# A list-scheduled Longformer-and-mixer kernel: a later second gather and other costs in its planner

## Chip, cores and metric

The kernel runs on one core of one Trainium2 chip. The metric is the device time of one execution in microseconds (us). Before the change it is 309.04 us, the median of three runs (308.41 to 309.81).

## The reference

Inputs are q, k and v (8 batches, 8 heads, S = 576 positions, D = 64), eight global positions, and four weight matrices. All of it is float32 in DRAM.

```python
scores = scale * np.matmul(q, k.transpose(0, 1, 3, 2))
mask = np.abs(pos[:, None] - pos[None, :]) <= window          # window = 32
mask = mask | is_global[:, None] | is_global[None, :]
scores = np.where(mask, scores, -1000000000.0)
attn = softmax(scores);  x = (attn @ v) as (B, S, H * D)      # 576 x 512 per batch
h = np.maximum(xt @ w_tok1, 0.0) @ w_tok2                     # 576 -> 256 -> 576, xt is x transposed
u = x + h.transpose(0, 2, 1)
h2 = np.maximum(u @ w_ch1, 0.0) @ w_ch2                       # 512 -> 1536 -> 512
return (u + h2).astype(np.float32)
```

## The kernel before, in words

**Stages.** The eight batches b = 0..7 go through the same stages, in float16 with float32 sums on TensorE (PE). q, k and v are loaded (lines 504 to 528) and cast on ScalarE (ACT) or VectorE (DVE) (L533, L536, L548); v also gets a copy shifted by 64 rows (L556). q and k are transposed, on PE for batches 0 to 2 (L568, with the copies to qT at L571 and to kT at L576, and for the last 64 positions L587, L589, L591), by DMA afterwards. Scores of the band are matmuls L675, their exponentials L685 on ACT, masked at L691 on DVE, with the columns of the global keys copied at L694; the global rows are L705 to L714. Sums and products with v are L722, L728, L742 and L755, divided and written to x by L782 to L791. The token MLP is L805 (relu L809 to L814), then L823 with the sum u at L836 and L839. The channel MLP needs u transposed: L850 on PE with the copy to uT at L852 for b < 3, a DMA transpose later. Its first product is L868 (twelve blocks j of four matmuls; relu L860 on ACT or L862 on DVE) and for the last 64 rows of two batches L880; its second product is L911. L919 adds u to that and writes one of three output buffers `osb` in turn, and L922 stores the buffer from GpSimd's queue. An L919 thus waits for the store of three tiles before.

**Two gathers.** The key and query rows at the global positions are fetched by indirect DMAs on GpSimd (POOL, L489). The first gather serves batches 0 to 3. The second serves batches 4 to 7: two DMAs each into `g_q` and `g_k`, cast to float16 at L619 (on DVE or ACT), transposed on PE at L623. Those transposes stand at about 130 us in the program.

**What sets the order.** Nothing runs when `op()` (L96) is called; it records an operation with the engines that may do it and their costs, a priority, what it reads and writes, its PSUM keys, and for a DMA a tuple `dma = (work, weight, lag, packets)` and a delay `late`. `run()` (L119) is a list scheduler: again and again it takes for each engine the earliest candidates, of these the one with the lowest priority number, and so fixes each engine's program order, the engine where two are allowed, and the PSUM bank (`slot`). `flow` and `land` model the three queues (G for GpSimd, S for SyncE, A for ACT), which share the DMA engines by weight. After the landing so found a consumer's data count as there only `late + LATE` later (from 36 us on). A matmul group whose `mode` differs from the one before is charged 0.095 us more. All of this happens while the kernel is built; on the chip each engine runs its fixed list and waits on semaphores.

Of the kernel before, what the change touches and what calls it, by code (L numbers as in the profile page):

```python
# [16 lines left out]
NT = 5  # L17
# [10 lines left out]
def kernel(  # L28
# [84 lines left out]
        ops.append(dict(opts=opts, pri=pri, fn=fn, deps=deps, ps=ps, new=new, dma=dma, mode=mode, late=late, behind=set(behind)))  # L113
        return i

    RING, LATE = 4096, 2.0
    LAT = {"P": 0.16, "A": 0.1, "V": 0.09, "G": 0.05, "S": 0.0, "K": 0.0}

    def run(free, look, hop, warm_until):  # L119
# [73 lines left out]
        while ready:  # L193
            cand = {}
            for i in ready:
                o = ops[i]
                t0, sl = 0.0, None
                if o["new"]:
                    sl = slot(o["new"][0], len(o["new"][1]), max([free["P"]] + list(at[i].values())))
                    if sl is None:  # L200
                        continue
                    t0 = max(t0, max(x[0] for x in sl))
                best = None
                for k, (e, c) in enumerate(o["opts"]):
                    st = max([free[e], t0] + [f + (hop if x != e else 0.0) for x, f in at[i].items()])
                    if o["dma"]:
                        ln, z = lanes["G" if e == "G" else "S"], filled["A" if e == "K" else e]
                        if len(ln) >= 8:
                            st = max(st, max(ln[-8], ln[-7], ln[-6]) + 2.5 if e == "A" else ln[-8])
                        room, x = RING - o["dma"][3], len(z)  # L210
                        while x and room >= z[x - 1][1]:
                            room -= z[x - 1][1]
                            x -= 1
                        if x:
                            st = max(st, z[x - 1][0])
                    if e == "P" and o["mode"] != mode:
# [12 lines left out]
            e, (st, _, i, c, sl) = pick  # L229
            o = ops[i]  # L230
            if e == "P":
                gap, spare = st - free["P"], [k for k in range(8) if (banks[k][1] is None or not open_uses[banks[k][1]]) and banks[k][0] <= free["P"]]
                if st < warm_until and gap > 0.52 and spare:
                    warm(min(spare, key=lambda k: (banks[k][0], k)), int((gap - 0.3) / (0.22 if st < 12.0 else 0.12)))
                mode = o["mode"]
            if o["new"]:
                kind, keys, shape, dt = o["new"]
                for key, (_, k) in zip(keys, sl):
                    home[key] = [k, k + 1] if kind == "S" else [k]
                    for z in home[key]:  # L240
                        banks[z] = (0.0, key)
                    ps_tile[key] = view(k, shape, dt)
            o["fn"](e)
            free[e] = st + c
            f = st + c + LAT[e]
            if o["dma"]:
                work, size, lag, packets = o["dma"]
                q = "A" if e == "K" else e
                if e == "A":
                    free["S"] = max(free["S"], st) + 0.9 * o["dma"][3] / 1024  # L250
                drain(min(f, min(free[x] for x in "GSA")))
                f = land(q, f, work, size, i)
                filled[q].append((f, packets))
                f += lag
                lanes["G" if e == "G" else "S"].append(f)
                f += o["late"] + (LATE if st > 36.0 else 0.3)
            fin[i] = f
            log.append((st, f, e, i, max(o["deps"], key=lambda x: fin[x]) if o["deps"] else None))
            ready.discard(i)
            for key in o["ps"]:  # L260
                open_uses[key] -= 1
                for z in home[key]:
                    banks[z] = (max(banks[z][0], f + hop), key)
            for u in users[i]:
# [227 lines left out]
                )  # L492
        return f

    TURN, STORE = (0.75, 256, 0.35, 544), (0.78, 2048, 0.8, 128)

# [7 lines left out]
    def load_qk(b, ti, hs, pri, opts, after=(), late=0.0, ):  # L504
        def f(e):
            ENG[e].dma_start(
                out=(lq, lk)[ti][:, hs].rearrange("p h i d -> p h (i d)"),
                in_=(q, k)[ti][b, hs, 0 : S - LAST, :].rearrange("h (p i) d -> p h (i d)", i=4),
            )
        ps_ = range(hs.start // 2, hs.stop // 2)  # L510
        op(opts, pri, f, w=[("l", ti, p) for p in ps_], dma=(0.75 * len(ps_), 4096, 2.0, 64) if opts[0][0] == "G" else ((0.75 if b else 0.95) * len(ps_), 1024, 1.2, 256 * len(ps_)), behind=after, late=late)

    def load_rest(b, pri, opts, after=(), late=0.0, ):
        for t, ten in enumerate((q, k)):
            def f(e, t=t, ten=ten):
                ENG[e].dma_start(
                    out=lr[LAST * t : LAST * t + LAST], in_=ten[b, :, S - LAST : S, :].rearrange("h p d -> p h d")
                )
            op(opts, pri, f, w=[("lr", t)], dma=(0.5, 4096, 2.0, 32) if opts[0][0] == "G" else (0.78 if b else 0.9, 256, 1.2, 512), behind=after, late=late)

    def load_v(b, pri, opts, after=(), late=0.0, ):
        for c in range(NT):
            def f(e, c=c):
                r0, r1, j0 = vrows(c)
                ENG[e].dma_start(
                    out=lv[r0:r1, c], in_=v[b, :, j0 : j0 + (r1 - r0), :].rearrange("h p d -> p h d")
                )
            op(opts, pri + 0.1 * c, f, w=[("lv", c)], dma=(0.9 if 0 < c < NT - 1 else 0.7, 4096, 2.0, 64) if opts[0][0] == "G" else (1.05 if 0 < c < NT - 1 else 0.8, 256, 1.2, 1024), behind=after, late=late)

    def cast_qk(b, ti, p, pri, opts):  # L530
        def f(e):
# [201 lines left out]
    def values(b, tau, pri, split):  # L733
# [29 lines left out]
            rl += [("vo", i, tau, 0), ("vo", i, tau, 1)]  # L763
        rg = [("lf", i), ("rf", i)]
        new = ("S", [key], [P, 2, 512], F32) if full else ("M", [key], [P, 512], F32)
        cl, cg = (0.27, 0.213) if full else (0.15, 0.12)
        if split:
            op([("P", cl)], pri, lambda e: local(True, False), r=rl + [("lf", i)], ps=[key], new=new, mode="c")
            op([("P", cg)], pri - 0.5, lambda e: [glob(hf, False, True) for hf in range(2)], r=rg, ps=[key], mode="c")
# [203 lines left out]
    for b in range(B):  # L973
# [3 lines left out]
            loads(b)  # L977
        if b == 0:
            n0 = len(ops) - 1
            op([("G", 1.0)], -176, f_w1, w=["w1"], dma=(1.7, 4096, 2.0, 512), behind=[n0])  # L980
            op([("G", 1.9)], -175, f_w1l, w=["w1l"], dma=(0.4, 4096, 2.0, 64), behind=[n0])
            n2 = len(ops) - 1
            op([("G", 0.77)], -173, f_wc1(0), w=[("wc1", 0)], dma=(2.6, 4096, 2.0, 512), behind=[n0])
            op([("G", 1.0)], -174.5, f_w2, w=["w2"], dma=(2.4, 4096, 2.0, 512), behind=[n0])
            for t in (1, 2):
                op([("G", 0.77)], -173 + t, f_wc1(t), w=[("wc1", t)], dma=(2.6, 4096, 2.0, 512), behind=[n0])
            n1 = len(ops) - 1
        if b == 1:
            op([("G", 1.2)], -18, lambda e: qk_pads(1, nc.gpsimd), w=[("qT", 1, p) for p in range(NP)] + [("kT", 1, p) for p in range(NP)] + [("qTr", 1), ("kTr", 1)], behind=[n1])
# [1 line left out]
            op([("G", 0.75)], -16, f_pads2(1), w=[("x", 1, NT - 1), ("lf", 1)])  # L991
        if b < 2:
            for ti in range(2):
                op([("G", 2.7)], (-115 if ti == 0 else -174.2) if b == 0 else 70, f_gather(b, ti), r=["idx"], w=[("g32", b, ti)], dma=(0.1, 256, 1.7, 256), late=0.0 if b or ti else 2.3,
                   behind=[] if b == 0 and ti == 0 else [n2])
        casts(b)
        cast_v(b, ca - 20, [("A", 0.52), ("V", 0.57)] if b < 2 else [("A", 0.52)])
        shift_v(b, ca - 19, [slice(0, 2), slice(2, 4)] if b == 0 else [slice(0, 4)])
        if b == 0:
            loads(1, n0)  # L1000
            op([("G", 0.77)], -40, f_wc2(0), w=[("wc2", 0)], dma=(2.6, 4096, 2.0, 512), behind=[len(ops) - 1])
            load_v(1, -39, [("G", 0.87)], [len(ops) - 1])
            n0 = len(ops) - 1
            for t in (1, 2):
                op([("G", 0.77)], -36 + t, f_wc2(t), w=[("wc2", t)], dma=(2.6, 4096, 2.0, 512), behind=[n0])
        if b == 1:
            glob_rows(0, slice(1, 4), ca - 40)
        if b == 4:
# [67 lines left out]
```

## Time and profile before

| | |
|---|---|
| profiled execution, device time | 308.4 us |
| its span, first to last instruction | 306.7 us |
| mean granted PE clock | 0.987 |
| median of three other runs | 309.04 us |
| PE busy | 289.9 us |
| DVE, ACT, POOL busy | 187.3, 178.9, 60.2 us |

The rows that the prediction quotes come from five views. The page gives busy time by engine. The windows view gives, for a stretch of the span, each engine's busy time with its instruction count, then the granted PE clock, the DMA share and GB/s. The timeline of an engine gives start, length, line, operation, `output<-inputs`, shapes and count; in square brackets stands how long the engine was idle before the row and what ended that. The DMA issues of a stretch give queue, kind, KB and the time from issue to landing. The view of one tile gives the smallest, middle and largest of these landing times. Rows marked `ACTq` are instructions that ACT issues to a DMA queue.

### The profile page before, as it was taken

What the parts mean: (1) busy time and instruction counts of PE and PEld (TensorE: products, weight loads), DVE (VectorE), ACT (ScalarE), POOL (GpSimd) and SP (SyncE); (2) the same over time, 40 slices, a digit from 0 to 9 for tenths busy, and PEclk for the clock granted to TensorE, in tenths of its full rate; (3) what the DMA queues carried; (4) which work ended last, traced back from release to release, by engine and by line L of the source; (5) the groups of instructions that cost most, each with busy time, mean ns of one, the idle gap of its engine ahead of it and who ended that gap; (6) DMA issues with size and microseconds to landing.
All of it is one profiled execution on the core that took longest, in us unless ns stands there. A gap on an engine that the chain in (4) does not pass through costs nothing. (4 is left out here: it accounts for less than half of the span.)

```text
span 306.7 us, 7290 instructions
## 1 busy us (share of the span) xinstructions
PE 289.9 (95%) x2955; PEld 154.9 (51%) x2955; DVE 187.3 (61%) x411; ACT 178.9 (58%) x325; POOL 60.2 (20%) x109
## 2 busy tenths in 40 slices
PE   5969989997999989999989999999999999999995
PEld 3746645444474444544456445444555445444643
DVE  7778866668786536994476655976587357230012
ACT  3873895376986369812996089714992183305600
POOL 8489635642001010002000100002000200020000
PEclk9798999999999999999999999999999999999999
DMA  6988999999997973499946995699844411071013
GB/s 170 257 137 272 220 226 212 298 214 301 193 149 139 309 205 62 96 163 230 311 76 131 218 338 143 98 214 220 288 100 90 135 38 37 8 148 69 0 71 104
DMA packets 94820, 51.31 MB, mean 167 GB/s; under 512 B 73730, under 2 KB 90242, under 8 KB 94786
## 3 DMA queue, kind: packets, MB, share of 16 engines
q1 hardware_dynamic: 62480, 26.36, 39.9%
q0 software_dynamic: 8704, 18.45, 24.1%
q10 hardware_dynamic: 23602, 6.03, 11.1%
q8 instruction: 23, 0.38, 0.5%
q14 instruction: 11, 0.09, 0.1%
HBM read 36.11 MB, written 9.44 MB: 149 GB/s over the span
## 5 line engine op out<-in xcount | busy, mean ns | idle before, releaser
L868 PE MATMUL bank<-uT,wc 128*128 128x512 f16 x384 | 92.3, 380 | 2.5 <-DVE qT L591 1.7
L911 PE MATMUL bank<-wc,b 128*128 128x512 f16 x384 | 87.5, 379 | 0.0
L685 ACT ACTIVATE e<-bank 128x648 f16<-128x648 f32 x64 | 42.9, 740 | 44.3 <-PE bank L675 43.2
L860 ACT ACTIVATE b<-bank 128x512 f16<-128x512 f32 x87 | 51.6, 620 | 26.3 <-PE bank L868 26.2
L911 PEld LDWEIGHTS <-b 128*128 128x128 f16 x384 | 36.8, 98 | 42.6
L868 PEld LDWEIGHTS <-wc 128*128 128x128 f16 x384 | 35.1, 98 | 43.5 <-issue 4.3
L922 POOL DMA_DIRECT2D out_dram<-osb x28 | 15.6, 556 | 198.6 <-DVE osb L919 198.6
L919 DVE TENSOR_TENSOR osb<-u,bank 128x512 f32<-128x512 f16 x32 | 21.9, 686 | 46.3 <-PE bank L911 46.1
L691 DVE TENSOR_TENSOR e<-e,masku 128x1296 f16<-128x1296 f16 x28 | 23.3, 832 | 20.5 <-ACT e L685 20.1
L548 ACT CAST vsh<-lv 128x512 f16<-128x512 f32 (+3 forms) x44 | 26.6, 621 | 7.5 <-DMA lv<-in_v_dram 7.1
L836 DVE TENSOR_TENSOR u<-x,bank 128x512 f16<-128x512 f16 x30 | 18.7, 682 | 8.1 <-PE bank L823 7.8
L783 DVE TENSOR_TENSOR x<-bank,rr 128x512 f16<-128x512 f32 x32 | 22.1, 692 | 1.1
L823 PE MATMUL bank<-a,w 128*128 128x512 f16 x80 | 19.9, 379 | 0.6 <-DVE a L811 0.4
L675 PEld LDWEIGHTS <-kT 64*128 64x128 f16 x576 | 11.3, 96 | 15.2 <-issue 14.1
L805 PE MATMUL bank<-x,w 128*128 128x512 f16 x64 | 18.7, 379 | 0.0
L536 ACT CAST qk<-lk 128x512 f16<-128x512 f32 x27 | 16.6, 627 | 1.7 <-DMA lk<-in_k_dram 1.7
L742 PE MATMUL bank<-rf,lf 128*64 128x264 f16 x144 | 16.1, 294 | 1.2 <-ACT b L860 0.9
L675 PE MATMUL bank<-qT,kT 64*128 64x72 f16 x576 | 15.6, 196 | 1.2 <-ACT e L685 1.2
L536 ACT CAST qk<-lq 128x512 f16<-128x512 f32 x26 | 15.8, 624 | 1.2 <-DMA lq<-in_q_dram 0.7
L755 PEld LDWEIGHTS <-e 128*64 128x64 f16 x576 | 16.1, 115 | 0.1
L755 PE MATMUL bank<-vsh,e 128*64 128x66 f16 x320 | 15.9, 198 | 0.0
L653 DVE COPY kT<-raw 128x512 f16<-128x512 f16 x20 | 12.0, 599 | 5.2 <-DMA raw<-qk 4.9
(166 smaller groups left out, 333.8 us busy)
## 6 DMA issues: line engine op xcount, KB each, us to landing
out_dram<-osb POOLq DMA_DIRECT2D x28, 256.0 KB, 4.3
lq<-in_q_dram SPq DMA_DIRECT2D x11, 512.0 KB, 7.0
lk<-in_k_dram SPq DMA_DIRECT2D x11, 512.0 KB, 9.2
lv<-in_v_dram ACTq DMA_DIRECT2D x15, 256.0 KB, 5.4
wc<-in_moe_w_ch_dram POOLq DMA_DIRECT2D x6, 512.0 KB, 13.3
lq<-in_q_dram POOLq DMA_DIRECT2D x4, 512.0 KB, 8.5
lk<-in_k_dram POOLq DMA_DIRECT2D x4, 512.0 KB, 9.8
lv<-in_v_dram ACTq DMA_DIRECT2D x10, 192.0 KB, 5.7
```

What stands on the lines that cost most here:

```text
L536: COPY[e](out=qk[:, ti, p].rearrange("q i (r d) -> q r i d", r=2), in_=(lq, lk)[ti][:, hs])
L548: COPY[e](out=vsh[i][a:z, c, :, 0:D], in_=lv[a:z, c])
L675: nc.tensor.matmul(ps_tile[keys[z]][:, u // 3, UW * (u % 3) : UW * (u % 3) + UW], lhsT=kT[r, 64 * u : 64 * u + P], rhs=qT[r, u // 2, UW * ...
L685: op([("A", 0.595)], pri + 1, lambda e, par=par: nc.scalar.activation(out=es[i][:, 2 * p + par].rearrange("p (n u) x -> p n u x", n=3), in ...
L691: op([("V", 0.85)], pri + 2, lambda e: nc.vector.tensor_mul(out=e2, in0=e2, in1=masku.unsqueeze(1).to_broadcast([P, 2, NB, UW])), r=["mask ...
L755: nc.tensor.matmul(o[:, VW * hh : VW * hh + VW], lhsT=es[i][:, h, 2 * tau + c, x : x + 64], rhs=vod[i][:, tau, h, :] if c else vsh[i][:, t ...
L783: nc.vector.tensor_tensor(out=xo, in0=pq[:, :, :, 0:D], in1=rr.unsqueeze(3).to_broadcast([P, 2, NP, D]), op=ALU.mult,)
L823: nc.tensor.matmul(ps_tile[key], lhsT=w2[:, ch, P * tau - sh : P * tau - sh + P], rhs=a1[:, ch, :], start=(ch == 0), stop=(ch == 1 and not ...
L860: nc.scalar.activation(out=out, in_=in_, func=AF.Relu)
L868: nc.tensor.matmul(ps_tile[key], lhsT=wc1[:, cc, P * j : P * j + P], rhs=uT[:, cc, :], start=(cc == 0), stop=(cc == 3))
L911: nc.tensor.matmul(ps_tile[key], lhsT=w, rhs=wc2[:, j, :], start=(j == 0), stop=(j == NJ - 1))
L919: nc.vector.tensor_add(out=osb, in0=uls[b // 2 % 2] if last else u16s[i][:, tau], in1=ps_tile[key])
```

## The change

The second gather gets `late = 12.0` instead of 0 and both gathers a weight of 128 instead of 256, so the planner counts the second gather's data as there 12 us later. `LATE` falls from 2.0 to 1.0 for all other loads. GpSimd's loads get a weight of 100000 (`BIG`) instead of 4096 in the queue model, and the loads of v on that queue 1.35 and 1.1 us of work instead of 0.9 and 0.7. A store gets a weight of 600 instead of 2048. The half-array products of the last tile (`cl`, `cg`: products with v for 64 rows) cost 0.19 and 0.15 instead of 0.15 and 0.12. The 0.095 us of a mode switch are charged only where mode "n" is left. No operation is added or removed by hand.

```diff
-    RING, LATE = 4096, 2.0
+    RING, LATE = 4096, 1.0
...
-                    if e == "P" and o["mode"] != mode:
+                    if e == "P" and mode == "n" != o["mode"]:
                         c = c + 0.095
...
-    TURN, STORE = (0.75, 256, 0.35, 544), (0.78, 2048, 0.8, 128)
+    TURN, STORE, BIG = (0.75, 256, 0.35, 544), (0.78, 600, 0.8, 128), 100000
...
-            op(opts, pri + 0.1 * c, f, w=[("lv", c)], dma=(0.9 if 0 < c < NT - 1 else 0.7, 4096, 2.0, 64) if opts[0][0] == "G" else (1.05 if 0 < c < NT - 1 else 0.8, 256, 1.2, 1024), behind=after, late=late)
+            op(opts, pri + 0.1 * c, f, w=[("lv", c)], dma=(1.35 if 0 < c < NT - 1 else 1.1, BIG, 2.0, 64) if opts[0][0] == "G" else (1.05 if 0 < c < NT - 1 else 0.8, 256, 1.2, 1024), behind=after, late=late)
...
-        cl, cg = (0.27, 0.213) if full else (0.15, 0.12)
+        cl, cg = (0.27, 0.213) if full else (0.19, 0.15)
...
-                op([("G", 2.7)], (-115 if ti == 0 else -174.2) if b == 0 else 70, f_gather(b, ti), r=["idx"], w=[("g32", b, ti)], dma=(0.1, 256, 1.7, 256), late=0.0 if b or ti else 2.3,
+                op([("G", 2.7)], (-115 if ti == 0 else -174.2) if b == 0 else 70, f_gather(b, ti), r=["idx"], w=[("g32", b, ti)], dma=(0.1, 128, 1.7, 256), late=12.0 if b else (0.0 if ti else 2.3),
```

The other loads and weights on GpSimd's queue get `BIG` in the same way. POOL's program order is the same before and after, and SyncE's almost. The orders of PE, DVE and ACT are the same for about the first 15 us and differ in many places behind that. 9 of the relus L860 on ACT become L862 on DVE (99 to 90, and 9 to 18), and two filler matmuls (L286) on zeros are gone from PE. Three places matter below.

**Place 1, DVE between batches 1 and 2.** The program order of VectorE at about 62 to 76 us; `osb_102` to `osb_104` are the three output buffers, `qT_72` and `kT_74` the transposed q and k of batch 2, `u_1_95` the sum of batch 1, `g_q_196` the second gather's rows. Before:

```order
L836 TENSOR_TENSOR u_1_95<-x_1_92,bank 128x512 x4
L919 TENSOR_TENSOR osb_102<-u_0_94,bank 128x512
L839 TENSOR_TENSOR ul_96<-x_1_92,bank 64x512
L619 CAST g_q_196<-g_q_192 128x128
L556 COPY vod_78<-vsh_76 64x2112
L919 TENSOR_TENSOR osb_103<-u_0_94,bank 128x512
L919 TENSOR_TENSOR osb_104<-u_0_94,bank 128x512
L556 COPY vod_78<-vsh_76 64x2112
L589 COPY kT_74<-bank 128x4x64
L591 COPY qT_72<-bank 128x4x64
L571 COPY qT_72<-bank 128x4x128 x2
L919 TENSOR_TENSOR osb_102<-u_0_94,bank 128x512
```

And now, in the same place:

```order
L919 TENSOR_TENSOR osb_102<-u_0_94,bank 128x512
L536 CAST qk<-lk 128x2x4x64
L919 TENSOR_TENSOR osb_103<-u_0_94,bank 128x512
L919 TENSOR_TENSOR osb_104<-u_0_94,bank 128x512
L836 TENSOR_TENSOR u_1_95<-x_1_92,bank 128x512 x4
L839 TENSOR_TENSOR ul_96<-x_1_92,bank 64x512
L556 COPY vod_78<-vsh_76 64x2112
L589 COPY kT_74<-bank 128x4x64
L919 TENSOR_TENSOR osb_102<-u_0_94,bank 128x512
L571 COPY qT_72<-bank 128x4x128 x3
```

The cast L619 of the gather is gone from here, to about 83 us, where the one of `g_k`, which stood on ACT, follows it. Three of the four adds L919 stand ahead of the four L836, and the fourth, which writes `osb_102` for the second time, stands ahead of all three copies L571. The first L868 of batch 1 now writes the PSUM bank that this fourth add reads, and waits for it.

**Place 2, ACT between batches 2 and 3.** The program order of ScalarE at about 97 to 113 us; L525 are the loads of batch 4's v (parts of 96, 128, 128, 128 and 96 rows), which ACT issues. Before:

```order
L814 ACTIVATE a_93<-bank 128x1024
L852 COPY uT<-bank 128x4x128 x3
L525 DMA lv<-in_v_dram 96x8x64
L852 COPY uT<-bank 128x4x128
L525 DMA lv<-in_v_dram 128x8x64 x3
L525 DMA lv<-in_v_dram 96x8x64
L548 CAST vsh_76<-lv 32x8x64
L548 CAST vsh_76<-lv 64x8x64
L685 ACTIVATE e_81<-bank 128x648 x2
```

And now:

```order
L814 ACTIVATE a_93<-bank 128x1024
L525 DMA lv<-in_v_dram 96x8x64
L525 DMA lv<-in_v_dram 128x8x64 x3
L852 COPY uT<-bank 128x4x128 x2
L525 DMA lv<-in_v_dram 96x8x64
L852 COPY uT<-bank 128x4x128 x2
L548 CAST vsh_76<-lv 32x8x64
L548 CAST vsh_76<-lv 64x8x64
L548 CAST vsh_76<-lv 128x8x64 x2
L685 ACTIVATE e_81<-bank 128x648 x2
```

Four of the five issues have moved ahead of all four copies L852, and two casts more stand ahead of the exponentials. On PE, one L911 group of six matmuls has moved ahead of the last L805, one L911 of batch 2's tiles now writes the bank that the third L852 reads, and the second scores L675 of batch 3 stand ahead of its L705.

**Place 3, DVE in batch 4.** The program order of VectorE at about 144 to 153 us; `b_100` is the relu's output. Before:

```order
L691 TENSOR_TENSOR e_80<-e_80,masku 128x1296
L694 COPY eg<-e_80 128x2x5x8
L714 TENSOR_TENSOR lf_83<-lf_83,mf 128x576
L691 TENSOR_TENSOR e_80<-e_80,masku 128x1296
L694 COPY eg<-e_80 128x2x5x8
```

And now:

```order
L691 TENSOR_TENSOR e_80<-e_80,masku 128x1296
L694 COPY eg<-e_80 128x2x5x8
L714 TENSOR_TENSOR lf_83<-lf_83,mf 128x576
L862 TENSOR_SCALAR b_100<-bank 128x512
L691 TENSOR_TENSOR e_80<-e_80,masku 128x1296
L694 COPY eg<-e_80 128x2x5x8
L862 TENSOR_SCALAR b_100<-bank 128x512
L691 TENSOR_TENSOR e_80<-e_80,masku 128x1296
```

Relus of ACT now stand here on DVE: three in batch 4, and two in batch 5 in the same way.

More of the change, by code (lines that the diff above doesn't have):

```diff
@@ L510, in load_qk @@
         ps_ = range(hs.start // 2, hs.stop // 2)
-        op(opts, pri, f, w=[("l", ti, p) for p in ps_], dma=(0.75 * len(ps_), 4096, 2.0, 64) if opts[0][0] == "G" else ((0.75 if b else 0.95) * len(ps_), 1024, 1.2, 256 * len(ps_)), behind=after, late=late)
+        op(opts, pri, f, w=[("l", ti, p) for p in ps_], dma=(0.75 * len(ps_), BIG, 2.0, 64) if opts[0][0] == "G" else ((0.75 if b else 0.95) * len(ps_), 1024, 1.2, 256 * len(ps_)), behind=after, late=late)
     def load_rest(b, pri, opts, after=(), late=0.0, ):
@@ L518, in f @@
                 )
-            op(opts, pri, f, w=[("lr", t)], dma=(0.5, 4096, 2.0, 32) if opts[0][0] == "G" else (0.78 if b else 0.9, 256, 1.2, 512), behind=after, late=late)
+            op(opts, pri, f, w=[("lr", t)], dma=(0.5, BIG, 2.0, 32) if opts[0][0] == "G" else (0.78 if b else 0.9, 256, 1.2, 512), behind=after, late=late)
     def load_v(b, pri, opts, after=(), late=0.0, ):
@@ L979 @@
             n0 = len(ops) - 1
-            op([("G", 1.0)], -176, f_w1, w=["w1"], dma=(1.7, 4096, 2.0, 512), behind=[n0])
-            op([("G", 1.9)], -175, f_w1l, w=["w1l"], dma=(0.4, 4096, 2.0, 64), behind=[n0])
+            op([("G", 1.0)], -176, f_w1, w=["w1"], dma=(1.7, BIG, 2.0, 512), behind=[n0])
+            op([("G", 1.9)], -175, f_w1l, w=["w1l"], dma=(0.4, BIG, 2.0, 64), behind=[n0])
             n2 = len(ops) - 1
-            op([("G", 0.77)], -173, f_wc1(0), w=[("wc1", 0)], dma=(2.6, 4096, 2.0, 512), behind=[n0])
-            op([("G", 1.0)], -174.5, f_w2, w=["w2"], dma=(2.4, 4096, 2.0, 512), behind=[n0])
+            op([("G", 0.77)], -173, f_wc1(0), w=[("wc1", 0)], dma=(2.6, BIG, 2.0, 512), behind=[n0])
+            op([("G", 1.0)], -174.5, f_w2, w=["w2"], dma=(2.4, BIG, 2.0, 512), behind=[n0])
             for t in (1, 2):
-                op([("G", 0.77)], -173 + t, f_wc1(t), w=[("wc1", t)], dma=(2.6, 4096, 2.0, 512), behind=[n0])
+                op([("G", 0.77)], -173 + t, f_wc1(t), w=[("wc1", t)], dma=(2.6, BIG, 2.0, 512), behind=[n0])
             n1 = len(ops) - 1
@@ L1000 @@
             loads(1, n0)
-            op([("G", 0.77)], -40, f_wc2(0), w=[("wc2", 0)], dma=(2.6, 4096, 2.0, 512), behind=[len(ops) - 1])
+            op([("G", 0.77)], -40, f_wc2(0), w=[("wc2", 0)], dma=(2.6, BIG, 2.0, 512), behind=[len(ops) - 1])
             load_v(1, -39, [("G", 0.87)], [len(ops) - 1])
@@ L1004 @@
             for t in (1, 2):
-                op([("G", 0.77)], -36 + t, f_wc2(t), w=[("wc2", t)], dma=(2.6, 4096, 2.0, 512), behind=[n0])
+                op([("G", 0.77)], -36 + t, f_wc2(t), w=[("wc2", t)], dma=(2.6, BIG, 2.0, 512), behind=[n0])
         if b == 1:
```

## The prediction

> **What bounds the kernel now.** I read the page first, for the busy times.
>
> ```profile
> span 306.7 us, 7290 instructions
> ...
> PE 289.9 (95%) x2955; PEld 154.9 (51%) x2955; DVE 187.3 (61%) x411; ACT 178.9 (58%) x325; POOL 60.2 (20%) x109
> ```
>
> PE works 289.9 of 306.7 us, so all idle time of PE together is 16.8 us, and a new order of the same matmuls can give back no more than this. The windows view tells where it lies.
>
> ```profile
> 70.00:80.00 10.00, 8.09 (x111) 4.40 (x108) 8.68 (x16) 7.90 (x17) 1.71 (x3) 1.00 1.23 235
> ...
> 110.00:120.00 10.00, 9.13 (x88) 4.39 (x87) 4.50 (x9) 9.94 (x20) 0.23 (x1) 1.00 0.37 104
> 150.00:160.00 10.00, 9.15 (x139) 5.04 (x137) 6.87 (x18) 9.91 (x19) 0.00 (x0) 1.00 0.68 173
> ```
>
> The first figure behind the stretch's length is PE. Much of PE's idle time lies in the first 15 us, where the orders are equal, and stays. 70 to 80 lacks 1.91. In 110 to 120 and in 150 to 160 PE lacks 0.87 and 0.85 while ACT (the fourth busy time) is full at 9.94 and 9.91: there PE waits for ACT. The timelines of PE, DVE and ACT name the waits around 73 us.
>
> ```profile
> 69.66 1.95 PE L568 MATMUL bank<-ident,qk 128*128 128x128 f16 x32
> 73.34 1.02 PE L868 MATMUL bank<-uT,wc 128*128 128x512 f16 x4 [1.73 <-DVE qT L591]
> 74.30 0.69 PE L675 MATMUL bank<-qT,kT 64*128 64x72 f16 x18
> ...
> 76.08 0.41 PE L705 MATMUL bank<-qT,kgz 128*32 128x512 f16 x4
> ...
> 77.42 0.47 PE L675 MATMUL bank<-qT,kT 64*128 64x72 f16 x18
> ```
>
> ```profile
> 69.73 0.23 DVE L619 CAST g_q<-g_q 128x128 f16<-128x128 f32 x1 [2.16 <-DMA g_q<-in_q_dram,idx_i]
> ...
> 74.40 0.68 DVE L919 TENSOR_TENSOR osb<-u,bank 128x512 f32<-128x512 f16 x1
> 75.00 0.68 DVE L571 COPY qT<-bank 128x512 f16<-128x512 f16 x1
> ```
>
> ```profile
> 71.85 0.30 ACT L619 CAST g_k<-g_k 128x128 f16<-128x128 f32 x1 [2.33 <-DMA g_k<-in_k_dram,idx_i]
> ```
>
> DVE stands 2.16 us and ACT 2.33 us before a cast of gathered rows that nobody reads until 130 us, and behind them wait the copies that PE needs: PE idles 1.73 at L868, its longest wait after 25 us.
>
> **The change, place 1.** With the casts at about 83 us those two waits go; each cast then costs 0.23 to 0.30 of DVE time and nothing to PE, as DVE is busy 61%. What is late next is the fourth add L919, now ahead of the L571 copies. It writes `osb_102` again and so waits until the first store has landed. The POOL timeline, the landing times and the view of all stores bound that:
>
> ```profile
> 64.18 0.94 POOL L489 DMA_INDIRECT g_k<-in_k_dram,idx_i  x1 [0.30 <-issue]
> 66.78 0.59 POOL L922 DMA_DIRECT2D out_dram<-osb  x1 [1.65 <-DVE osb L919]
> ```
>
> ```profile
> g_k<-in_k_dram,idx_i POOLq DMA_INDIRECT x1, 7.6
> ```
>
> ```profile
> out_dram<-osb POOLq DMA_DIRECT2D x1, 256.0 KB, 7.4
> ```
>
> ```profile
> DMA to landing us min/median/max: 2.3/4.3/9.9
> ```
>
> The last gather is issued at 64.18 and lands at 71.8; the store issued at 66.78 lands at 74.2, 2.4 behind it, which is about the shortest landing of any store (2.3): its data moved only once the gather's were through. POOL's order is unchanged, so the earlier first add can bring the store's issue forward to 65.1 (64.18 + 0.94) and no further, still behind the gather. I take it to land at 74.2 again; the bounds are 72.6 (landing 7.4 after an issue at 65.2) and, with two more stores right behind it, about 75. The add then ends at 74.2 + 0.1 + 0.68 = 75.0, and L868 starts there instead of at 73.34. From L868 to L705 before needs 2.74, of which 0.22 is the first scores' wait for qT (0.69 against 0.47 at 77.42) and about as much the pause behind it; without those 2.3 are left, and L705 starts at 77.3 instead of 76.08: **+1.2**, with bounds −0.5 and +2.
>
> PE also comes to this wait sooner. Twelve matmuls L911 have moved up to 50 to 55 us, ahead of waits such as these:
>
> ```profile
> 46.14 3.61 PE L868 MATMUL bank<-uT,wc 128*128 128x512 f16 x16 [0.55 <-ACT b L860]
> ...
> 50.35 0.24 PE L722 MATMUL bank<-vsh,eg 128*32 128x132 f16 x4 [0.25 <-ACT vsh L548]
> ...
> 51.83 0.42 PE L742 MATMUL bank<-rf,lf 128*64 128x264 f16 x4 [0.27 <-DVE rf L728]
> ```
>
> That gains 0.52 at 50 to 52 us, and 1.1 if the wait at 46 us goes with them, but the store wait swallows it all: PE now stands idle from about 70.5 (71.6, the end of L568, less 1.1) to 75.0. A clock follows from this. The granted clock is the number behind the five busy times, and it changes in steps of 3.41 us:
>
> ```profile
> 18.54:21.96 3.42, 1.68 (x41) 0.89 (x37) 2.32 (x7) 3.04 (x7) 2.81 (x4) 1.00 0.94 124
> 21.96:25.37 3.41, 3.37 (x80) 3.27 (x82) 2.57 (x7) 0.30 (x1) 3.41 (x6) 0.52 0.65 129
> 69.74:73.16 3.42, 1.87 (x34) 1.75 (x32) 3.31 (x7) 1.06 (x3) 1.17 (x2) 1.00 1.08 354
> 73.16:76.57 3.41, 3.05 (x35) 1.33 (x35) 2.90 (x6) 3.41 (x7) 0.54 (x1) 1.00 2.02 252
> ```
>
> A step in which PE was busy 1.68 was followed by one at 0.52; a step with 1.87 by one at full clock. With PE out from 70.5 the step from 69.74 holds about 0.8 of work (at most 1.35, were only 0.52 gained), so the next one, to 76.57, should be at half clock. PE works in it from 75.0 on, 1.6 us at half speed: **+0.8**. Bounds: 0, if the steps lie otherwise in that run, and 2.5, if that step in its turn counts as too empty and the next is halved as well (1.7 more). The Trainium skill, page "TensorE: Matmul & The Clock Gate", section "Part 1: The HAM clock gate (the 'warmup' mystery)", has a free-running window of 3413 ns, which the rows bear out, and a fall to half clock after at least one idle window. The row of 18.54 speaks against the second, since a window half full was enough. By the page 4.5 us need not hold one whole idle window, there would be no fall, and the sum below would be 0.8 less; the row decides.
>
> **Place 2.** ACT's timeline of batch 3, with the loads' largest issue time and two landing times of them:
>
> ```profile
> 97.15 1.02 ACT L814 ACTIVATE a<-bank 128x1024 f16<-128x1024 f32 x1 [0.87 <-PE bank L805]
> 100.69 1.90 ACT L852 COPY uT<-bank 128x512 f16<-128x512 f16 x3 [2.52 <-PE bank L850]
> 102.06 0.34 ACTq L525 DMA_DIRECT2D lv<-in_v_dram  x1
> ```
>
> ```profile
> 104.70 4.88 ACTq L525 DMA_DIRECT2D lv<-in_v_dram  x2
> ```
>
> ```profile
> L525 ACTq DMA_DIRECT2D lv<-in_v_dram x25: 337/409/3702, 69.0 to 206.7; - x25
> ```
>
> ```profile
> lv<-in_v_dram ACTq DMA_DIRECT2D x1, 192.0 KB, 6.4
> ```
>
> ```profile
> lv<-in_v_dram ACTq DMA_DIRECT2D x1, 192.0 KB, 11.1
> ```
>
> An issue takes 0.34 to 0.41, but the fourth of five took up to 3.70: it stuck until the first load had landed (102.1 + 6.4 = 108.5). Before, ACT had nothing urgent behind it. Now four issues stand right behind L814 and ahead of the copies L852, and PE needs the third of those. L814 ends 1.29 later than before (one L911 of six matmuls now ahead of the last L805), at 99.5; the first load lands at 99.5 + 6.4 = 105.9; then two copies (0.63 each, by 1.90 for three), one issue and the third copy: 108.2. PE, with the 1.29 and without a wait of 0.56, is there at 105.3:
>
> ```profile
> 100.26 0.40 PE L850 MATMUL bank<-ident,u 128*128 128x128 f16 x4 [0.56 <-DVE u L836]
> ...
> 103.32 5.34 PE L911 MATMUL bank<-wc,b 128*128 128x512 f16 x24
> ...
> 111.66 0.19 PE L675 MATMUL bank<-qT,kT 64*128 64x72 f16 x1 [0.40 <-ACT e L685]
> 112.26 0.45 PE L675 MATMUL bank<-qT,kT 64*128 64x72 f16 x17 [0.41 <-ACT e L685]
> 112.75 1.89 PE L868 MATMUL bank<-uT,wc 128*128 128x512 f16 x8
> ```
>
> (103.32 + 1.29 − 0.56, and 1.3, by 5.34 for 24, for a first L911 group of six, which need not wait.) It idles 3.0, to 108.3. Then come two L911 groups with scores between (1.3 + 0.4 + 1.3), and the second scores wait for the exponentials behind four casts: they end at about 112.2, and with L705 and eight L868 PE has at 114.5 done what it had done at 112.75 before: **+1.7**. Bounds: −1.4 if ACT isn't held (the idles 0.56, 0.40 and 0.41 gone), and +6.4 if the first load takes 11.1 instead of 6.4. For the clock here I take 0: its idle may fall into two steps (bound 0.8 as above).
>
> **Place 3.** In batches 4 and 5 five relus leave the full ACT for DVE, busy 6.87 of 10 there, and their L868 stand ahead of the products with v. The two waits there go:
>
> ```profile
> 156.67 0.30 PE L742 MATMUL bank<-rf,lf 128*64 128x264 f16 x2 [0.85 <-ACT b L860]
> ...
> 187.19 0.47 PE L722 MATMUL bank<-vsh,eg 128*32 128x132 f16 x20 [0.37 <-ACT b L860]
> ```
>
> **−1.2**, bounds −1.2 and 0.
>
> **The rest** costs nothing: the other figures only feed the planner, POOL's order is the same, and PE has the same products. From 15 to 35 us PE waits for landings and for DVE's division, which keep their order. I take 0 there.
>
> Sum: 1.2 + 0.8 + 1.7 − 1.2 = +2.5. The profiled execution took 308.4, so 310.9; the median of the plain runs stands 0.64 above it, so **311.5**. An effect below 0.5% (1.5 us) is about what a measurement of this kernel can't tell from no change.
>
> **Rivals.** *Faster:* the first store lands before about 72.5, from which point the fourth add ends before 73.3, where L868 started before, because its data needn't wait for the gather's; and ACT isn't held, the queue having room. For it: stores usually land in 4.3, which gives 69.5 from 65.2. Against it: the 7.4 and 3.70 of the rows. Then 1.73 + 0.43 at place 1, 1.37 at place 2 and 1.2 at place 3 are gained: −4.7, or **304.3**. *Cancelled:* place 1 holds but the clock doesn't fall, and at place 2 the hold and the saved waits are even: +1.2 − 1.2, **309.0**. *Worse:* the first load of v lands after 11.1, as it did for the load issued at 69 us, beside the gathers; against it, that the load issued at 102.06 took 6.4. Place 2 is +6.4, the sum +7.2, **316.2**.
>
> **How the numbers follow.** Forecast, both holds: 0.45 (309.8 to 313.5 by its bounds). Faster: 0.18. Cancelled: 0.25. Worse: 0.12. Faster by over 0.5% (below 307.5) is the faster case and the low end of the cancelled: 0.21. Within 0.5%: most of the cancelled and the low end of the forecast, 0.28. Slower: the rest and the worse, 0.51. The range reaches from 306.0, cutting most of the faster case, to 315.5.
>
> **What would show it.** In the changed trace L919 should wait for the store's landing at about 74 with L868 behind it, and the step after that idle should have a clock near 0.5; near 105 us L525 on ACT should take over 3 us with L852 behind it and PE idle 3 us at an L911; the waits at 156 and 187 should be gone. The forecast is wrong if the store lands well before 73, or if ACT's four issues take 0.4 each.

## The result, and the profile after

The changed kernel takes 318.37 us (median of six runs, 315.99 to 320.44), the kernel before 308.92 us on the same chip (six runs, 308.15 to 310.51). The ratio is 1.030, with a 95% interval of 1.024 to 1.036: slower by 3%, above the range that was given. Its profiled execution took 317.04 us with a span of 315.3 us, 8.6 us more than before.

The page of the changed kernel:

```profile
span 315.3 us, 7286 instructions
...
PE 291.8 (93%) x2953; PEld 156.1 (50%) x2953; DVE 194.2 (62%) x420; ACT 174.9 (55%) x316; POOL 59.6 (19%) x109
```

PE has the same work (291.8 us busy against 289.9); 6.7 of the 8.6 us are idle time of PE. To see where it comes in, I added up the matmuls in PE's order without the fillers, each at its median spacing in the trace of before, and compared the moments at which two kernels had done the same amount. That is the lag behind the kernel before, in us; the first column is the time in the trace of before. The other columns are kernels of the experiments.

```
before at  changed  e3     e9     e6     e7     p1
   33.8     2.22    0.50   0.89   0.18   0.32  -0.44
   68.7     0.87   -0.11  -0.47  -0.68  -1.04   1.04
   76.6    -0.42   -0.30  -0.37   0.26  -3.22   0.49   place 1
   97.8    -0.42   -0.30  -0.37   0.26  -3.18   0.49
  115.7     3.29    4.54  -2.10  -1.48  -4.91   0.05   place 2
  131.8     2.66    3.91  -0.72  -1.36  -4.80   0.49
  136.9     6.34    4.90   2.80   0.35  -3.23   1.93   place 4
  153.5     7.09    5.65   3.55   1.10  -2.49   1.93
  159.7     5.92    4.48   2.38  -0.07  -3.66   1.71   place 3
  202.1     6.03    4.60   2.53   0.44  -2.94   2.41
  207.1     8.16    5.08   2.53   0.93  -2.45   8.60   place 5
  300.3     8.64    5.57   3.01   1.41  -1.98   8.78
```

The changed kernel is 2.2 late after the start, has won that back by 77 us, and then loses 3.1 at place 2, 3.7 at a place 4 and 2.1 at a place 5 that the prediction did not have. The PE timeline at these places, where before had 1.73 at place 1 and at most 0.56 at the others:

```profile
73.33 1.04 PE L868 MATMUL bank<-uT,wc 128*128 128x512 f16 x4 [0.86 <-ACT kT L576]
...
107.76 1.46 PE L911 MATMUL bank<-wc,b 128*128 128x512 f16 x6 [2.84 <-ACT uT L852]
...
112.17 0.45 PE L675 MATMUL bank<-qT,kT 64*128 64x72 f16 x17 [1.02 <-ACT e L685]
...
139.81 1.46 PE L911 MATMUL bank<-wc,b 128*128 128x512 f16 x6 [1.59 <-DVE u L836]
143.05 5.34 PE L911 MATMUL bank<-wc,b 128*128 128x512 f16 x24 [1.78 <-DVE osb L919]
...
212.91 5.34 PE L911 MATMUL bank<-wc,b 128*128 128x512 f16 x24 [1.78 <-DVE osb L919]
```

What stood before those rows: DVE at place 1 (the row names ACT's copy L576, which ended at the same time as DVE's add, both at 73.3), then ACT at place 2, then DVE at places 4 and 5.

```profile
72.58 0.69 DVE L919 TENSOR_TENSOR osb<-u,bank 128x512 f32<-128x512 f16 x1 [1.14 <-DMA out_dram<-osb]
73.19 1.88 DVE L571 COPY qT<-bank 128x512 f16<-128x512 f16 x3
```

```profile
98.03 5.44 ACTq L525 DMA_DIRECT2D lv<-in_v_dram  x4
103.57 1.07 ACT L852 COPY uT<-bank 128x512 f16<-128x512 f16 x2 [4.52 <-DVE kT L653]
106.33 0.69 ACTq L525 DMA_DIRECT2D lv<-in_v_dram  x1
107.12 1.07 ACT L852 COPY uT<-bank 128x512 f16<-128x512 f16 x2 [2.48 <-DMA lq<-in_q_dram]
```

```profile
138.34 0.59 DVE L656 COPY qT<-raw 128x512 f16<-128x512 f16 x1 [2.40 <-DMA raw<-qk]
138.85 0.19 DVE L635 COPY qT<-gT 128x160 f16<-128x160 f16 x1
139.07 2.48 DVE L836 TENSOR_TENSOR u<-x,bank 128x512 f16<-128x512 f16 x4
...
208.30 0.60 DVE L656 COPY qT<-raw 128x512 f16<-128x512 f16 x1 [2.28 <-DMA raw<-qk]
208.94 2.48 DVE L836 TENSOR_TENSOR u<-x,bank 128x512 f16<-128x512 f16 x4
```

At place 2 the issues of loads of v hold ACT until 103.5 and again until 107.0, although the first row of L852 names DVE, which had long been done. Their own times (smallest, middle and largest, in ns), and a load that SyncE (SP) had issued before them:

```profile
L525 ACTq DMA_DIRECT2D lv<-in_v_dram x5: 374/637/747, 98.0 to 106.3; - x5
...
97.88 0.66 SPq L516 DMA_DIRECT2D lr<-in_k_dram  x1
...
lr<-in_k_dram SPq DMA_DIRECT2D x1, 128.0 KB, 5.1
```

None of the five issues was long. The 5.44 of the four together is mostly a wait ahead of the fourth, from 100.0 to 103.0, for a semaphore on which SyncE's load L516 counts as well: it ended as that load landed (97.88 + 5.1). In the same way the fifth waited until 106.3, when SyncE's load L506 of q landed, and the third copy L852, which PE needs, stands behind the fifth.

At places 4 and 5 DVE stands before a copy out of a DMA transpose (L656) that nobody needs for some us, and behind it wait the sums u (L836), for which PE waits. At place 5 this order is new: before, the L836 of batch 5 began at 200.64 and that copy stood behind them, at 206.33. At place 4 it is not. DVE in the kernel before, and the landing of the transpose that this copy reads:

```profile
133.20 0.60 DVE L656 COPY qT<-raw 128x512 f16<-128x512 f16 x1
133.83 2.48 DVE L836 TENSOR_TENSOR u<-x,bank 128x512 f16<-128x512 f16 x4
...
raw<-qk SPq DMA_TRANSPOSE x1, 2.4
```

There the copy stood ahead of the sums too, without a wait, as its transpose had landed 2.4 us after its issue. In the changed kernel that transpose was issued at 133.37 and landed at 138.3, after 4.9 us.

### The profile page after: what moved, and what is told of

It reads as the page before. It is cut to its first block, busy times and chain, and to the rows that moved or that the text cites. A ratio compares the mean times of both kernels' runs of the same rounds, so it can differ in the third digit from the quotient of the medians.

```text
span 315.3 us, 7286 instructions
## 1 busy us (share of the span) xinstructions
PE 291.8 (93%) x2953; PEld 156.1 (50%) x2953; DVE 194.2 (62%) x420; ACT 174.9 (55%) x316; POOL 59.6 (19%) x109
## 4 chain that ended last, share of the span: by engine, by line
PE 61%; DMA 12%; ACT 12%; DVE 9%; issue 3%; SPq 2%; ACTq 0%
PE bank L868 21%; PE bank L911 20%; DMA lv<-in_v_dram 6%; PE bank L805 4%; ACT vsh L548 4%; ACT e L685 3%; PE bank L823 3%; DMA raw<-qk 3%; PE bank L880 3%; PE bank L675 2%; DVE x L783 2%; PE bank L742 2%; ACT b L860 2%; PE bank L755 2%; DMA lr<-in_k_dram 2%
## 5 line engine op out<-in xcount | busy, mean ns | idle before, releaser
L911 PE MATMUL bank<-wc,b 128*128 128x512 f16 x384 | 88.8, 379 | 8.0 <-DVE osb L919 3.6
L868 PE MATMUL bank<-uT,wc 128*128 128x512 f16 x384 | 92.3, 380 | 1.4 <-ACT kT L576 0.9
L860 ACT ACTIVATE b<-bank 128x512 f16<-128x512 f32 x78 | 47.3, 614 | 31.3 <-PE bank L868 31.2
L911 PEld LDWEIGHTS <-b 128*128 128x128 f16 x384 | 36.6, 98 | 51.1 <-issue 9.4
L919 DVE TENSOR_TENSOR osb<-u,bank 128x512 f32<-128x512 f16 x32 | 22.0, 687 | 57.5 <-PE bank L911 54.9
L868 PEld LDWEIGHTS <-wc 128*128 128x128 f16 x384 | 35.0, 98 | 42.3 <-issue 2.4
L836 DVE TENSOR_TENSOR u<-x,bank 128x512 f16<-128x512 f16 x30 | 18.7, 682 | 5.7 <-PE bank L823 5.5
L675 PEld LDWEIGHTS <-kT 64*128 64x128 f16 x576 | 11.9, 98 | 17.2 <-issue 16.7
L536 ACT CAST qk<-lk 128x512 f16<-128x512 f32 x28 | 17.4, 636 | 2.3 <-DMA lk<-in_k_dram 2.3
L805 PE MATMUL bank<-x,w 128*128 128x512 f16 x64 | 18.5, 379 | 0.1
L675 PE MATMUL bank<-qT,kT 64*128 64x72 f16 x576 | 16.3, 199 | 2.0 <-ACT e L685 2.0
L656 DVE COPY qT<-raw 128x512 f16<-128x512 f16 x20 | 11.8, 600 | 6.9 <-DMA raw<-qk 6.9
```

The costliest lines, as they stand in the source:

```text
L536: COPY[e](out=qk[:, ti, p].rearrange("q i (r d) -> q r i d", r=2), in_=(lq, lk)[ti][:, hs])
L675: nc.tensor.matmul(ps_tile[keys[z]][:, u // 3, UW * (u % 3) : UW * (u % 3) + UW], lhsT=kT[r, 64 * u : 64 * u + P], rhs=qT[r, u // 2, UW * ...
L805: nc.tensor.matmul(ps_tile[key][:, tt], lhsT=w, rhs=x16s[i][:, ch, :], start=(ch == 0), stop=(ch == NT - 1))
L860: nc.scalar.activation(out=out, in_=in_, func=AF.Relu)
L868: nc.tensor.matmul(ps_tile[key], lhsT=wc1[:, cc, P * j : P * j + P], rhs=uT[:, cc, :], start=(cc == 0), stop=(cc == 3))
L911: nc.tensor.matmul(ps_tile[key], lhsT=w, rhs=wc2[:, j, :], start=(j == 0), stop=(j == NJ - 1))
```

## The experiments

Most kernels here keep the planner's list of before or after and move single entries of it, so that nothing else changes place. The edit that they share (the moves are written as operation, target, 0 for ahead of it or 1 for behind):

```diff
-            o["fn"](e)
+            plan.append((i, e, 0))
...
+        for x, to, behind in MOVES:
+            step = plan.pop([z[0] for z in plan].index(x))
+            plan.insert([z[0] for z in plan].index(to) + behind, step)
+        for i, e, n in plan:
+            warm(e, n) if i < 0 else ops[i]["fn"](e)
```

The theory after the result: the loss is made by two holds, a load issue stuck on ACT ahead of uT and a copy waiting for a transpose ahead of the sums on DVE, put there by the planner's new figures. The rivals: the later gather itself, a late start, or data that come late in any order.

**e1, the title of the change alone.** In the list of before, the two casts L619 behind batch 3's L648 and L650:

```diff
-MOVES = []
+MOVES = [(670, 531, 1), (671, 670, 1)]
```

> The kernel before with its order written out, and in it only the two casts L619 of the second gather moved to about 83 us: the title of the change, alone. Theory (the gather's wait was real, and the losses of the changed kernel come from the other figures): PE's wait of 1.73 us before L868 at 73 us falls below 0.6, and the whole is about 1.3 us faster, ratio 0.996 (0.994 to 0.998). Rival (the landing of the first store is next late and takes the place of the gather): the wait stays over 1.3, ratio 0.999 to 1.002.

Ratio 1.0025 (0.9985 to 1.0066): the rival. The gather's wait is gone, and DVE and PE show the next in line:

```profile
74.74 0.69 DVE L919 TENSOR_TENSOR osb<-u,bank 128x512 f32<-128x512 f16 x1 [1.97 <-DMA out_dram<-osb]
```

```profile
75.48 1.02 PE L868 MATMUL bank<-uT,wc 128*128 128x512 f16 x4 [2.21 <-DVE osb L919]
```

**e2, which of two readers of one PSUM bank comes first.** In the list of after, kT's copy of batch 0 is recorded ahead of qT's again:

```diff
+MOVES = [(77, 78, 0)]
```

> The changed kernel, with one thing put back: of the two copies out of the same PSUM bank for heads 4 and 5 of batch 0 (kT by L576 on ACT, qT by L571 on DVE), kT's is recorded first again; no engine's own order differs. Theory (two engines that read one PSUM bank wait for one another in the order in which they were recorded, and in the changed kernel ACT waits for DVE, which waits for v): ACT's L576 at 15.8 starts at about 14.3, PE's waits of 1.01 and 0.87 at 16.4 and 17.6 fall to 0.4 and 0.3, and the lag of 2.2 us that the changed kernel has at 30 us falls to 0.3: ratio to the kernel before 1.023 instead of 1.030, so about 316.2. Rival (the start was late for another reason, the landings of the first loads): lag at 30 us still over 1.5, ratio 1.027 or more.

Ratio 1.035 (1.029 to 1.042), lag at 34 us 1.8: a miss. The two waits of PE at the masks fell to 0.63 and 0.26, but the first loads landed later in this run and longer waits followed. The start scatters from run to run: in the eight profiles with the start of after the lag at 34 us is 0.2 to 2.2 (mean 0.9), in the five with that of before −0.7 to 1.0 (mean 0). About 1 us may be the order's; one profile of each does not settle it.

**e3, the copies behind the sums at places 4 and 5.**

```diff
+MOVES = [(693, 595, 1), (822, 693, 1), (991, 897, 1)]
```

> The changed kernel, in which at two places one copy L656 out of a DMA transpose's result (and one L635) stands behind the sums L836 and L839 on DVE again instead of ahead of them, in batches 3 and 5. Theory (DVE waits 2.4 and 2.3 us there for the transposes and holds the sums u, for which PE's L911 wait 1.59 + 1.78 and 1.78 us; the smaller LATE put the copies there): those three PE waits go, 5 us in all, ratio about 1.014, some 313. Rival (the transposes are late anyway and their copies then hold the adds L919 or the scores instead): PE waits as long a few us later, ratio 1.024 or more.

Ratio 1.020 (1.014 to 1.025), against 1.030 for the changed kernel and between theory and rival. In the lag table place 5 costs 0.5 instead of 2.1, with a transpose as late as before (4.8 us), so the hold there was real. Place 4 costs 1.0 instead of 3.7, but in this profile its transpose landed after 2.4 us, so the copy would have waited little in either place; e9 and e6 settle that one. Place 2 cost 4.8 up to 115.7 us instead of 3.7, with a step at half clock behind the wait.

**e4, two of the loads behind uT.**

```diff
+MOVES = [(652, 445, 1), (653, 652, 1), (665, 547, 1), (666, 557, 1), (668, 669, 0)]
```

> The changed kernel, with ACT's last two loads L525 of batch 4's v behind the four copies L852 of batch 2, and two casts L548 behind the exponentials of batch 3. Theory (the fourth issue stuck on ACT until the first load had landed, and held uT): PE's wait of 2.84 at 107.8 goes, and of those of 1.02, 0.15, 0.27 and 0.41 behind it no more than 0.8 is left; ratio about 1.018, some 314.6. Rival (the exponentials are late anyhow, as in the kernel before, and take what is gained): the wait at L911 goes, but those at the scores grow to 3 us or more, ratio 1.027 or more.

A copy of v on DVE (L556) moves with the casts, here and in e6 and e9.

Ratio 1.026 (1.020 to 1.032), near the rival. uT comes in time, but the fifth issue now sticks, and a cast behind it waits for v, both ahead of the exponentials. ACT, then PE:

```profile
98.43 2.09 ACTq L525 DMA_DIRECT2D lv<-in_v_dram  x3
...
105.92 4.64 ACTq L525 DMA_DIRECT2D lv<-in_v_dram  x1
110.60 1.89 ACT L548 CAST vsh<-lv 32x512 f16<-32x512 f32 x3 [5.69 <-issue]
```

```profile
113.14 0.69 PE L675 MATMUL bank<-qT,kT 64*128 64x72 f16 x17 [4.59 <-ACT e L685]
```

Here the issues themselves last, 1.55 for the fourth and 4.64 for the fifth. So it was not enough to move them past uT: nothing that sticks may stand ahead of the exponentials either.

**e6, both holds undone.** Issues four and five and three casts go behind exponentials, with e3's moves:

```diff
+MOVES = [(652, 542, 1), (653, 552, 1), (664, 547, 1), (665, 653, 1), (666, 557, 1), (668, 669, 0),
+         (693, 595, 1), (822, 693, 1), (991, 897, 1)]
```

> The changed kernel with the copy L656 behind the sums in batches 3 and 5, as in the run before it, and with ACT's fourth and fifth load of batch 4's v behind the first two and four exponentials L685 of batch 3, and the casts of its second to fourth part later still. Theory (what the changed kernel loses in the middle are two holds of an engine's own making: a stuck load issue or a cast that waits for v ahead of what PE needs on ACT, and a copy that waits for a transpose ahead of the sums on DVE): PE's waits between 105 and 117 us together fall below 1.2, the lag behind the kernel before at 131 us is below 0.5, the transposes of batch 4's q and k are issued some 3 us earlier for it, the waits at L911 near 140 and 210 fall below 0.6 each, ratio 1.002 (0.996 to 1.008). Rival (the data themselves come too late in this order, so each hold is followed by another): ratio 1.014 or more, with waits of over 2 us left behind 100 us.

Ratio 0.998 (0.994 to 1.001). Nine entries moved in the list of the changed kernel take away the whole 3%. On PE no wait is left between 75 and 118 us; one of 1.56 at L911 near 137, over the 0.6 expected, and one at place 1 remain:

```profile
74.00 1.04 PE L868 MATMUL bank<-uT,wc 128*128 128x512 f16 x4 [3.07 <-DVE osb L919]
...
118.16 0.47 PE L722 MATMUL bank<-vsh,eg 128*32 128x132 f16 x20 [0.68 <-ACT b L860]
137.05 3.18 PE L911 MATMUL bank<-wc,b 128*128 128x512 f16 x14 [1.56 <-DVE osb L919]
```

**e9, the ACT half of e6 alone.**

```diff
+MOVES = [(652, 542, 1), (653, 552, 1), (664, 547, 1), (665, 653, 1), (666, 557, 1), (668, 669, 0)]
```

> The changed kernel with only the loads and casts of batch 4's v behind the exponentials of batch 3; the copies L656 stay ahead of the sums. Theory (place 2 makes ACT late with the casts of batch 4, SP's transposes late behind those, and so DVE's wait ahead of the sums in batch 3 longer): the lag at 131 us is below 0, the growth near 137 us below 2 instead of 3.7, that near 207 stays at 2 to 3.4; ratio 1.012 (1.005 to 1.019). Rival (the copies wait for their transposes wherever those start): 3 us or more are lost near 137, ratio 1.020 or more.

Ratio 1.014 (1.008 to 1.021), as expected in the whole, but not in its parts: the lag falls below 0 at 131 us, and yet DVE waits 1.85 for the transpose near 135 and 3.5 is lost there, while place 5 costs nothing this time: its transpose landed after 2.5 us. SP's transposes did start 3.1 us sooner than in the changed kernel (seven from 122.53 instead of 125.64), but the sums came sooner as well. Place 4 is therefore a hold of its own, not a consequence of place 2. The transpose there landed after 4.8 us in e9 and 4.6 in e6; with the copy ahead of the sums 3.5 was lost, with it behind them 1.7. One half gives 1.5%, the other (e3) 1.0%, both 3.2%.

**e8 and e10, the store behind the gather.** A fourth output buffer in the kernel before, with the casts late (e8) and without (e10):

```diff
-    osbs = [const.tile([P, DM], F32, name=f"osb{i}") for i in range(3)]
+    osbs = [const.tile([P, DM], F32, name=f"osb{i}") for i in range(4)]
...
-        osb = osbs[o]
+        osb = osbs[(nout[0] - 1) % 4]
```

> The kernel before with the casts L619 at about 83 us, as in the first run, and a fourth output buffer: the fourth add L919 then waits for no store. Theory (behind the gather it was the first store's landing that held PE at 73 to 75 us): PE's wait at L868, 2.21 us in the first run and 1.73 before, falls below 0.8, ratio 0.995 (0.991 to 0.998). Rival (the copies of qT and kT are late for themselves): the wait stays over 1.3, ratio 0.999 to 1.003.

> The kernel before with a fourth output buffer and nothing else. Theory (gather and first store end within half a microsecond of one another there, and either holds PE alone): PE's wait at L868 near 73 us stays at 1.4 to 1.8, ratio 0.999 (0.996 to 1.002). Rival (the store alone held it): the wait falls below 0.8, ratio 0.995 or less.

e8: ratio 0.992 (0.988 to 0.997), wait at L868 0.38. e10: ratio 0.9985 (0.995 to 1.002), wait 1.51. PE in e8, then in e10:

```profile
72.08 1.02 PE L868 MATMUL bank<-uT,wc 128*128 128x512 f16 x4 [0.38 <-DVE qT L591]
```

```profile
73.14 1.02 PE L868 MATMUL bank<-uT,wc 128*128 128x512 f16 x4 [1.51 <-DVE qT L591]
```

Later casts alone (e1): nothing. A buffer alone (e10): nothing. Both: 0.8%. Two things held the same place until nearly the same moment.

**e7, the same buffer on top of e6.** The diffs of e6 and e8 together.

> The changed kernel with both holds undone (the loads and casts of batch 4's v behind the exponentials, the copy L656 behind the sums), and a fourth output buffer. Theory (with the holds gone, place 1 is left, where L919 waits for the first store and PE 3.07 us for L919): PE's wait at L868 near 73 us falls below 1.0, ratio 0.991 (0.987 to 0.996), below the kernel before. Rival (what comes early at place 1 is lost again to landings behind it): the wait goes and the ratio stays at 0.997 to 1.001.

Ratio 0.9895 (0.986 to 0.993), median 306.34 us against 309.49 for the kernel before beside it: 1% faster than the kernel before. PE at place 1 goes from L568 to L868 without a wait:

```profile
68.79 1.78 PE L568 MATMUL bank<-ident,qk 128*128 128x128 f16 x29
70.42 1.04 PE L868 MATMUL bank<-uT,wc 128*128 128x512 f16 x4
```

**p1, p2 and p4, which figure.** The planner run with one figure changed in before, or put back in after:

```diff
p1  -    RING, LATE = 4096, 2.0
    +    RING, LATE = 4096, 1.0
p2  -    RING, LATE = 4096, 1.0
    +    RING, LATE = 4096, 2.0
p4  -    late=12.0 if b else (0.0 if ti else 2.3)
    +    late=0.0 if b or ti else 2.3
```

> The kernel before, planned with LATE = 1.0 and no other new figure. In its program order the loads of batch 4's v stand where they stood before. Theory (it takes LATE together with the other figures to put loads ahead of uT and copies ahead of the sums): ratio 1.001 (0.996 to 1.007), no new wait of PE over 1 us. Rival (LATE = 1.0 alone makes DVE or ACT wait for data that are not there yet): ratio 1.015 or more.

> The changed kernel, planned with LATE = 2.0 as before and all other new figures. In its program order ACT's loads of batch 4's v stand behind two and four of the copies L852, no longer ahead of all; one copy L656 still stands ahead of the sums in batch 3. Theory (LATE put the loads there): no wait of PE over 0.6 at L911 near 107, and the lag does not grow between 98 and 120 us by more than 1, while that near 137 stays; ratio 1.010 (1.002 to 1.018). Rival (the other figures cost the time whatever LATE is): ratio 1.024 or more.

> The changed kernel, planned with the second gather's late = 0 as before and all other new figures. In its program order the casts L619 follow DVE's three copies L571 at 75 us, the loads of v stand ahead of uT on ACT and a copy L656 ahead of the sums, as in the changed kernel. Theory (the later gather is not what costs the time): ratio 1.029 (1.020 to 1.038). Rival (it is the later gather that upsets the plan): ratio 1.012 or less.

p4: 1.024 (1.017 to 1.031), so the later gather is not what costs the time. p1: 1.016 (1.008 to 1.024), the rival, and against my theory: LATE = 1.0 alone costs half of the loss. In its profile 6.2 us of lag come in at one place near 207, where PE waits 3.18 for sums that DVE holds and works at half clock from 208.2 to 215.0:

```profile
209.21 9.48 PE L911 MATMUL bank<-wc,b 128*128 128x512 f16 x30 [3.18 <-DVE u L836]
```

```profile
211.59:215.01 3.42, 3.42 (x9) 1.22 (x8) 1.70 (x4) 0.00 (x0) 0.54 (x1) 0.50 0.83 187
```

p2: 1.014 (1.006 to 1.022), but its four runs lie far apart (309.60, 311.63, 314.96 and 315.84 us). Its profile, taken of the first, ends 1.2 late; the copy of place 5 stands behind the sums again, and at neither place do the sums wait for a transpose. In p1 they wait 1.75 near 136 and 1.86 near 208. So in these profiles LATE is what makes the holds on DVE. How much of the time stays with LATE put back, and which of the remaining figures makes it, is open.

## Why the prediction was wrong, point by point

**The step that failed** is "The rest costs nothing: the other figures only feed the planner, POOL's order is the same, and PE has the same products." The figures feed the planner, and LATE tells it when loaded and transposed data are there. In the new plan DVE, which serves its list in order, waits at two places for a transpose ahead of the sums: at place 5 because a copy L656 moved ahead of them, at place 4 because the transpose for a copy that stood there before as well took 2.5 us longer to land. I followed three places in the new order and took the others as unchanged, because no wait stood there before. The lag table has +3.7 at place 4 and +2.1 at place 5, of +8.6 in all; e3 shows for place 5, and e6 beside e9 for place 4, that the copy ahead of the sums makes it, and e6 that with place 2 they are the whole loss. How much place 4 costs changes from run to run: with the same order, the lag grew by only 0.8 there in e2, where the transpose landed after 2.4 us.

**Place 1, +1.2.** Mechanism right, size wrong. L919 does wait for the store and holds the copies, and with it PE (e1, e6). But the store had landed by 72.6 (L919 started at 72.58), my lower bound, not at 74.2, and L868 began at 73.33, as before. In the seven profiles with this order it began between 72.4 and 74.0: about 0, not 1.2. L705 began at 75.67, 0.4 sooner than before, where I had it 1.2 later. PE came to the place later, being late from the start, and so waited only 0.86 there.

**The clock, +0.8 at place 1 and 0 at place 2.** At place 1 the wait was too short for it. At place 2 the 0 held in the changed kernel, but not in e2, e3, e4 and p4, where PE waited 3.15, 4.72, 4.59 and 4.23. Steps of 3.41 us in the changed kernel, then in e2 (the first figure behind the length is PE, the granted clock follows POOL):

```profile
106.12:109.53 3.41, 1.77 (x24) 0.82 (x23) 0.00 (x0) 2.36 (x5) 0.36 (x1) 1.00 1.12 359
109.53:112.94 3.41, 2.24 (x34) 1.14 (x32) 0.87 (x2) 2.40 (x4) 0.54 (x1) 1.00 1.07 271
```

```profile
105.40:108.81 3.41, 0.55 (x3) 0.29 (x3) 0.43 (x1) 1.18 (x3) 0.54 (x1) 1.00 1.11 360
108.81:112.23 3.42, 3.42 (x26) 1.28 (x24) 0.00 (x0) 2.71 (x5) 0.00 (x0) 0.50 1.14 303
```

A step with 1.77 busy is followed by full clock, one with 0.55 by half. In the Trainium skill, page "TensorE: Matmul & The Clock Gate", section "Part 1: The HAM clock gate (the 'warmup' mystery)", the fall needs an idle window; the row of e2 shows a fall behind one that was not quite idle, and the measurement decides. The steps begin at other moments in each run, so nearly the same wait costs a clock step in one and none in another: 3.15 in e2 cost one; 3.07 at place 1 in e6 cost none, as it fell into two steps, with 1.71 and 2.04 of work.

**Place 2, +1.7.** The hold was right and its reason wrong. PE waited 2.84 against 3.0 forecast at the L911 named, and the scores behind it 1.02. But I had the fourth issue stick until the first load of v landed, at 105.9, and the fifth pass at once. In the changed kernel the fourth took 0.37 and stood until 103.0 for the landing of SyncE's load, and the fifth, which I had as free, until 106.3 for another; the two made up the 3.0 by luck. The issues that did last are in e2, e3 and p4 (1.8 to 2.9 for the fourth, behind the same wait of 1.2). The lag grew by 3.1 from 98 to 131 us, between the 1.7 and the bound of 6.4.

**Place 3, −1.2.** The waits at the L742 of batch 4 and the L722 of batch 5 are gone, and the lag falls from 7.09 to 5.92. But little of this is a gain: just ahead of it the lag had grown from 6.34 to 7.09, as PE waits 0.30 and 0.15 for exponentials near 155, and in batch 5 it waits 0.33 at an L868 near 188. Over the two batches about 0.3 is left of the 1.2. The forecast counted the waits that go and none that come.

**The start, 0.** Too confident: 2.2 in this profile, about 1 as a mean, and not settled. The clock has a share in it: between 17 and 28 us two steps are at half clock in the changed kernel, one in the kernel before, and none in e6 (lag 0.2).

## What to carry to other kernels

A planner's figure for when data arrive is part of the schedule: where engines serve fixed lists, an entry placed 1 us too early is a wait for everything behind it, so follow every load and transpose in the new order to what stands behind its first consumer, not only the places that wait now or whose order has changed. Where two things hold a place until the same moment, taking one away shows nothing until the other goes too. And ahead of what the busiest engine needs, put nothing that can stick, not even the issue of a load: it can last, and it can stand behind the landing of another engine's load.

## What the runs showed of the hardware

The first three issues of loads on ACT's queue took 2.0 to 2.1 us together in e4 and e6; one more right behind them can last (3.70 in the kernel before, 4.64 in e4), and ACT computes nothing meanwhile.

A DMA transpose issued together with loads landed later. For the transpose that the copy at place 4 or 5 reads this holds in all 14 profiles (before, changed, and the twelve experiments): issued 0.82 us or less ahead of ACT's first load of v, or just behind it, it landed after 4.1 to 5.1 us (19 cases); issued 0.85 us or more ahead, after 2.4 to 2.5 (9 cases). No run moved those loads alone, so it is not shown that they are the cause.

Two engines that read one PSUM bank wait for one another here in the order in which the program recorded them: in the changed kernel ACT's copy L576 waits 1.44 at 15.8 us for DVE's copy L571 of the same bank, with neither engine's own order changed there; in e2, recorded the other way round, it starts without a wait.

```profile
15.79 1.07 ACT L576 COPY kT<-bank 128x512 f16<-128x512 f16 x2 [1.44 <-DVE qT L571]
```
